# When rider queries, extra keys and LayerNorm rows are transposed in a segment-recurrent attention kernel, and how its instruction pages are counted

## The chip, the cores and the metric

The kernel runs on one core of one Trainium2 chip. The metric is the device time of the whole program in microseconds: a median over several executions. A core has TensorE (matmuls, which write to PSUM), VectorE, ScalarE, GpSimd and SyncE; the last two issue most of the DMA transfers here. Each engine runs its own instruction stream in order, and the streams meet only at semaphores.

## What is computed

The reference is one transformer layer on 2048 tokens of width 640. Its first half is an attention with a recurrent memory: the tokens are cut into 64 segments of 32, each is preceded by 8 memory rows, and the first 8 rows of a segment's attention output are the memory of the next one. So the segments have to be done one after the other. Its second half is a gated feed-forward block.

```python
mem = mem0                                             # 8 rows
for s in range(64):
    h = concatenate([mem, layernorm(x)[32*s : 32*s+32]])   # 40 rows of 640
    q, k, v = h @ Wq, h @ Wk, h @ Wv                   # 32 heads of 128
    p = softmax(mask(q @ k.T / sqrt(128)))
    o = (p @ v) @ Wo
    mem = o[:8]
    outs.append(o[8:])
h = x + concatenate(outs)
out = h + (relu(n @ W_gate) * (n @ W_up)) @ W_down     # n = layernorm(h)
```

## The kernel before

All weights of the attention stay in SBUF. The program is written out in full, segment by segment (the loop at L895), into a list of operations with what each reads and writes. `solve` derives the semaphore waits from that list, and every engine then runs its own operations in the order in which they were added. So the order of the source is the order of each engine, and the order of the SyncE queue in particular is the order in which the DMAs were added.

**One step.** The only thing that depends on the step before is the memory: 8 rows. A matmul on 8 rows costs TensorE as much as one on 32, so the other 24 columns of each projection pass carry "riders": LayerNorm rows of tokens that come one to three segments later. Segment s projects memory s and 24 rider tokens. Four steps bring 96 rider tokens but use up 128, and the missing 32 of every 128 are projected as "extra tokens" in the gaps of three of four steps (`extra_units`, L848): their keys when s % 4 is 2, their queries when it is 3, their values when it is 0. "Kind" below is s % 4.

A step runs on TensorE in this order: K projection into banks 0 and 1, Q projection, first part of the V projection, `pick_mem` (L447, takes the memory queries out of the Q tokens), rest of V, `scores` (L560), the extra projection in five parts (`filler`, L966) with the memory's attention between them, `wo_pass` (L636, the output projection, 128 short matmuls at L642, which gives the next memory), then `pv_x` (L670), the attention of the 32 tokens.

**Token buffers and transposes.** A projection comes out with tokens on the partitions, while scores need the head dimension there. So each result is copied out of PSUM into a token buffer (`to_tok`, L427) and transposed by a DMA on the SyncE queue (`dma_t`, L360). There are four buffers of 512 columns: K goes through `tok` 0 and 1 into `KS`, Q through `tok` 2 and 3 into `QS`. ScalarE copies the even buffers and VectorE the odd ones. From `KS` and `QS` the riders' part is copied into the rings `Kr` and `Qr` (`evac_k`, `evac_q`), where they wait for their segment. `KS` itself is read by this step's scores. The extra tokens' keys and queries are copied by ScalarE into `tok` 2 and 3 (`evac`, L864) and transposed into `Kr` or `QS`.

**When the queries' transpose is issued.** `trans_q` (L456) is issued early, right after the Q copies, in steps of kinds 2 and 3. In kinds 0 and 1 (`qlate`, L938) it is issued after the step's output projection and the first copy of the new memory (L1000), and its copy into `Qr` follows in the next step (`late_k`).

**LayerNorm rows.** Rows of x are loaded into `xt`, scaled by VectorE (`row_scale`, L985), and transposed into `at` (L1005), from where GpSimd copies them into the passes' operand buffers (`ln1_back`). This happens in kind 2, and in kind 0 after steps 31, 35, 39 and 43 for rows of the second half of the layer (`e2b`). `at` also holds, earlier in kinds 1 and 2, the sum of an extra output projection on its way to memory.

**Instruction pages.** TensorE's instructions are fetched in pages of 256 (`PE_LINE`). A matmul is two instructions (weight load and multiply) or, where it keeps its weights, one. `align` (L136) walks through TensorE's operations, keeps the count `at`, and turns some kept weights back into loads (`spare`), so that a page boundary falls a set number of instructions (`MARKS`) after the start of each step's output projection. Waits count too: an instruction can carry one wait, and the others go into separate instructions of up to two waits each. `align` counts one for every wait after the first.

Of the kernel before, what the change touches and what calls it, by code (L numbers as in the profile page):

```python
# [41 lines left out]
class _Graph:  # L42
# [93 lines left out]
    def align(self, first, line):  # L136

        at, spare = first, []  # L140
        for op in self.ops:
            if op.eng != "pe":
                continue
            if op.mark is not None:
                p = (-(at + op.mark)) % line
                room = sum(o.spare[1] for o in spare)
                if p <= room:
                    at += p
                    for o in reversed(spare):
                        o.spare[0] = min(p, o.spare[1])  # L150
                        p -= o.spare[0]
                spare = []
            c = _Count()
            op.fn(c)
            at += c.n + max(0, len(op.waits) - 1)
            if op.spare is not None:
                spare.append(op)

# [48 lines left out]
def build_kernel(nc, A_x, A_mem0, A_Wq, A_Wk, A_Wv, A_Wo, A_seg_len, B_W_gate, B_W_up, B_W_down, out):  # L207
# [15 lines left out]
    VW = 130  # L223
    RING = 96
    PE_FIRST, PE_LINE = 64, 256
    MARKS = (150, 98, 114, 130)

    x_ap, out_ap, mem0_ap = A_x[0], out[0], A_mem0[0]
    h_d = nc.dram_tensor("h_d", [TB, D], BF16)
# [74 lines left out]
    BQ = (0, 1)  # L304
# [55 lines left out]
    def dma_t(dst, src, r, w):  # L360
        add("sp", lambda e: e.dma_start_transpose(dst, src), r=r, w=w, dma=True)
# [65 lines left out]
    def to_tok(b, t, eng):  # L427
        copy_op(eng, tok[t][:, :], bank(b), [B(b)], [("tok", t)])
# [419 lines left out]
    def extra_units(s):  # L848

        b, r = (s - 2) // 4, (s - 2) % 4
        t0 = 64 + 128 * b + 96
        if b < 0 or r == 3 or t0 >= S:
            return None, None, None
        a, ks = act_e[b % 2], [("acte", b % 2)]
        q = seg_slot(t0 // SEG)
        j = (1, 0, 2)[r]

        def part(n):
            project(a, ks, j, (0, 1), BQ, PARTS[n], j // 2)

        def evac():  # L864
            for i, e in enumerate(("act", "act")):
                if j == 2:
                    to_v(BQ[i], Vr[q], i, ("Vr", q), e)
                else:
                    to_tok(BQ[i], 2 + i, e)
            if j == 1:  # L870
                dma_t(Kr[q][:].rearrange("p h t -> p (h t)").rearrange("p (k r) -> p k r", r=128), tokp[1][:, :],
                      [("tok", 2), ("tok", 3)], [("Kr", q)])

        def fin():
            trans_q()
            late_q.append(lambda: evac_q(QS, ("QS",), t0, 32, 0, "act"))
        return part, evac, (fin if j == 0 else None)
# [17 lines left out]
    for s in range(NSEG):  # L895
        last = s == NSEG - 1
        q = seg_slot(s)
        nb = s // 4 + 1
        ln = 64 + 128 * nb < S

        e2 = EARLY.index(s // 4 * 4 + 3) if s // 4 * 4 + 3 in EARLY else None
        e2b = EARLY.index(s - 1) if s - 1 in EARLY else None
        def loads(s=s, e2=e2, e2b=e2b, nb=nb, ln=ln):
            if s % 4 == 3 and e2 is not None:
                dma(xt[:, :], x_ap[128 * e2:128 * e2 + 128, :], r=[("KS",)], w=[("xt",)])
                load_attn(at, e2, [], ("at",))
            if s % 4 == 0 and ln and e2b is None:
                ln1_load(nb, xt, ("xt",))
            if s % 4 == 1 and s - 2 in EARLY:
                e = EARLY.index(s - 2)  # L910
                dma(xn2_d[e], at[:, :], r=[("at",)], w=[("xn2_d", e)])
                if ln:
                    ln1_load(nb, xt, ("xt",))
        if s == 0:
            loads()
        if s > 0:
            a, ks, kn = pass_act(s)
            t0, nr = rider_tokens(s)
            project(a, ks, 1, (0, 1), BQ, (0, 1), spare=16)
            ks = ks + kn  # L920
            project(a, ks, 1, (0, 1), BQ, (2, 3, 4), spare=24)
            to_tok(BQ[0], 0, "act")
            to_tok(BQ[1], 1, "dve")
            if last:
                break
            dma_t(KS[:].rearrange("p h t -> p (h t)").rearrange("p (k r) -> p k r", r=128), tokp[0][:, :],
                  [("tok", 0), ("tok", 1)], [("KS",)])
            trans_ox()
            for f in late:
                f()  # L930
            late = []
            project(a, ks, 0, (0, 1), (P0, P1), spare=40)
            to_tok(P0, 2, "act")
            to_tok(P1, 3, "dve")
            for f in late_k + late_q:
                f()
            late_k, late_q = [], []
            qlate = nr and s % 4 < 2  # L938
            if nr and not qlate and s < NSEG - 2:
                trans_q()  # L940
            loads()
            project(a, ks, 2, (0, 1), (P2, P3), (0, 1), spare=16)
            if s == NSEG - 2:
                trans8(tok[2], ("tok", 2), tok[3], ("tok", 3), T0)
                copy_op("dve", Qr[:, :, q, 0:M], slots(T0, 0, M), [B(T0)], [("Qm", q)])
                evac_q(slots(T0, 0, SEG), B(T0), t0, nr, M, "act")
            else:
                pick_mem(T0)
                copy_op("dve", Qr[:, :, q, 0:M], bank(T0)[:, 0:256].rearrange("p (h t) -> p h t", t=M), [B(T0)], [("Qm", q)])
            if nr:  # L950
                evac_k(KS, ("KS",), t0, nr, M, "dve")
            project(a, ks, 2, (0, 1), (P2, P3), (2, 3, 4), spare=24)
            to_v(P3, Vp, 1, ("Vp", 3), "dve")
            to_v(P2, Vp, 0, ("Vp", 0), "act", 0, 2)
            scores(s)
            exp_mem()
            to_v(P2, Vp, 0, ("Vp", 1), "act", 2, 4)
            exp_x()
            if nr:
                v_riders(t0, nr)  # L960
                if s < NSEG - 2 and not qlate:
                    evac_q(QS, ("QS",), t0, nr, M, "act")
        units, evac, nfin = extra_units(s)
        woe = s % 4 == 1 and s >= 5

        def filler(n):  # L966
            if units:
                units(n)
            if woe:
                woe_pass(BQ[0], WPARTS[n])  # L970
        filler(0)
        filler(1)
        pv_mem(s)
        if s % 4 == 1 and s >= 5:
            copy_op("dve", oTn[:, :, :], oT[:, :, 0:M], [("oT", "m"), ("oT", "n")], [("oTn",)])
        elif s > 0:
            copy_oTe(s - 1)
        norm_om()
        filler(2)
        filler(3)  # L980
        trans_om(128 if s % 4 < 2 else 32)
        mask_x()
        n = n_rows(nb) if s % 4 == 2 and ln else 128 if e2b is not None else 0
        if n:
            row_scale(xt, ("xt",), n, xt, ("xt",))  # L985
        filler(4)
        if evac:
            evac()
        if woe:
            copy_op("dve", oTe[:, :, 0:M], oTn[:, :, :], [("oTn",)], [("oTe", 0)])  # L990
            woe_sum(BQ[0])
            late.append(lambda b=s // 4 - 1: woe_store(b, [("KS",)]))
        wo_pass(T1, MARKS[s % 4] if s > 0 else None)
        if s == NSEG - 2:
            load_gate_up([("oTe", (s - 1) % 4), ("go", T1, 0)])
        to_act(s + 1, B(T1), bank(T1)[:, 0:160])
        if s >= 1:
            wo_rows(T1, wtok[s % 2], ("wtok", s % 2), "act")
            store_attn(wtok[s % 2], ("wtok", s % 2), s - 1)
            if qlate and s < NSEG - 2:  # L1000
                trans_q([("act", (s + 1) // 4 % 2, (s + 1) % 4, "m")])
                late_k.append(lambda t0=t0, nr=nr: evac_q(QS, ("QS",), t0, nr, M, "act"))
        pv_x(s, P0)
        if n:
            dma_t(chunks_of(at[:, :])[:, :, 0:n], xt[0:n, :], [("xt",)], [("at",)])  # L1005
            if s % 4 == 2:
                late.append(lambda nb=nb: ln1_back(nb, chunks_of(at[:, :]), [("at",)], "pool"))
        if nfin:
            nfin()
        norm_x(P0)  # L1010
        if s % 4 == 1 and ln:
            late.append(lambda nb=nb: row_stats(xt, ("xt",), n_rows(nb)))
        if s % 4 == 3 and e2 is not None:
            def f(e2=e2):
                add_attn(xt[:, :], xt, at, [("xt",), ("at",)], [("xt",)])
                dma(h_d[128 * e2:128 * e2 + 128, :], xt[:, :], r=[("xt",)], w=[("h_d", e2)])
                row_moments(xt, ("xt",), 128)
            late.append(f)
            late_q.append(lambda: row_rstd(128))
# [204 lines left out]
```

The softmax here doesn't subtract the row's maximum and nothing guards it: scores larger than these inputs give would overflow.

## Time and profile before

The three timed executions took 1107.77, 1101.67 and 1106.10 us; the median is 1106.1. The profiled execution's span is 1105.2 us, at a mean granted clock of 0.992.

| part of the page | what it says |
|---|---|
| largest TensorE groups | projections L420 and L398, 401.1 and 361.8 us; output projection L642, 156.5 us in 8064 matmuls of 234 ns |
| SyncE's transposes | QS 76, KS 62, oT 62, at 19, Kr 15, xn2T 12 |
| DMA queues | SyncE's own queue 265,776 packets, 41.6% of the 16 engines' span; GpSimd's queue 19,312 packets, 9.5% |
| GpSimd's transfers | Vr<-Vp 376, attn_d<-wtok 62, attn_d<-at 32 |
| chain that ended last | projections 24% and 24%, output projection 13%, FFN gate and up 11%; KS<-tok 2% |

In the lines of groups, the count after x is the number of instructions, then comes the time in which at least one of them ran, then the mean length of one in ns. A transpose is shown on SPq, SyncE's queue, with the time that its issue took; when its data has landed is told separately. "Idle before <- X" is the time that an engine stood still before an instruction and what seems to have ended it; "issue" means that the profile shows nothing that it waited for. Several groups of matmuls run side by side on 32 columns each, so the length of one matmul is not the distance between two.

### The profile page before, as it was taken

Reading aid. Unit: us, or ns where it says so; the run is one execution under the profiler, and the core shown is the slowest. Engines: PE = TensorE matmul, PEld = TensorE weight load, DVE = VectorE, ACT = ScalarE, POOL = GpSimd, SP = SyncE. Lnnn points to the kernel's source line nnn. Section 1 sums busy time; section 2 is a strip of 40 time slices with the busy share of each in tenths; the row PEclk is TensorE's granted clock in tenths of the full one; section 3 lists DMA queues with packets and bytes.
Section 4 is the critical chain, followed back from the end, with each engine's and each line's share of the span. In section 5 each row is a group of like instructions: output and inputs, shape, how many; then the busy total and the mean of one; then the engine's idle time right before and its main releaser. Section 6 shows DMA issues by size and latency. Waiting matters only on the chain.

```text
span 1105.2 us, 55764 instructions
## 1 busy us (share of the span) xinstructions
PE 1054.6 (95%) x27862; PEld 505.9 (46%) x23270; DVE 608.0 (55%) x1673; ACT 362.9 (33%) x792; POOL 290.8 (26%) x585
## 2 busy tenths in 40 slices
PE   4689999999999999999999999999999989999998
PEld 3344444454544444444454444444444455444443
DVE  3245656565656565666666666555656553563422
ACT  1214343333333333333333333333333332131220
POOL 1023333332323232323232324242324152000000
PEclk9989999999999999999999999999999999999999
DMA  9936464545465546567566666464555557222100
GB/s 362 388 92 111 87 104 89 104 91 102 89 100 93 100 89 105 95 107 114 109 111 113 105 117 107 96 99 84 94 108 95 79 148 249 43 78 78 25 18 25
DMA packets 285739, 121.61 MB, mean 110 GB/s; under 512 B 261376, under 2 KB 275156, under 8 KB 285504
## 3 DMA queue, kind: packets, MB, share of 16 engines
q1 hardware_dynamic: 265776, 93.92, 41.6%
q0 software_dynamic: 19312, 23.86, 9.5%
q8 instruction: 201, 3.29, 1.2%
q14 instruction: 34, 0.28, 0.1%
q10 hardware_dynamic: 416, 0.26, 0.1%
HBM read 36.79 MB, written 7.19 MB: 40 GB/s over the span
## 4 chain that ended last, share of the span: by engine, by line
PE 90%; DMA 5%; SPq 3%; issue 1%; DVE 1%; ACT 0%; DVEq 0%
PE ps L420 24%; PE ps L398 24%; PE ps L642 13%; PE ps L1036 11%; PE ps L680 3%; PE ps L656 3%; PE ps L570 3%; PE ps L1068 3%; SPq L358 3%; DMA Wo<-in_A_Wo_dram 3%; PE ps L607 2%; DMA KS<-tok 2%; PE ps L451 2%; PE ps L622 1%; PE ps L1091 1%
## 5 line engine op out<-in xcount | busy, mean ns | idle before, releaser
L420 PE MATMUL ps<-W,act_r 128*32 128x512 bf16 x4261 | 401.1, 387 | 6.6 <-DMA W<-in_A_Wv_dram 2.7
L398 PE MATMUL ps<-W,act_r 128*32 128x512 bf16 x3619 | 361.8, 379 | 1.5 <-issue 1.5
L358 POOL DMA_DIRECT2D Vr<-Vp x376 | 187.2, 505 | 353.3 <-ACT Px L589 288.4
L420 PEld LDWEIGHTS ps<-W,act_r 128*32 128x32 bf16 x4261 | 120.6, 98 | 263.6 <-issue 173.2
L462 ACT ACTIVATE tok<-ps 128x512 bf16<-128x512 f32 x192 | 110.9, 594 | 231.6 <-PE ps L398 205.3
L642 PE MATMUL ps<-Wo,oT 128*32 128x160 bf16 x8064 | 156.5, 234 | 11.2 <-DMA Wo<-in_A_Wo_dram 6.3
L464 DVE CAST tok<-ps 128x512 bf16<-128x512 f32 x131 | 90.6, 691 | 129.7 <-PE ps L398 111.0
L642 PEld LDWEIGHTS ps<-Wo,oT 128*32 128x32 bf16 x8064 | 142.7, 97 | 32.1 <-DVE oT L464 16.9
L420 PE MATMUL ps<-W,act_e 128*32 128x512 bf16 x900 | 90.0, 381 | 2.6 <-issue 2.6
L398 PE MATMUL ps<-W,act_e 128*32 128x512 bf16 x900 | 89.4, 379 | 0.0
L553 DVE STREAM_TRANSPOSE TBf<-ps 128x64 f32<-128x64 f32 (+1 forms) x128 | 33.6, 263 | 94.6 <-PE ps L642 94.6
L695 DVE TENSOR_TENSOR ox<-ps,rx 128x512 bf16<-128x512 f32 x128 | 82.5, 686 | 2.2
L358 POOL DMA_DIRECT2D attn_d<-wtok x62 | 46.3, 748 | 133.0 <-ACT wtok L462 133.0
L462 ACT ACTIVATE Qr<-QS 128x512 bf16<-128x512 bf16 (+3 forms) x107 | 69.7, 680 | 33.1 <-DMA QS<-tok 32.8
L462 ACT ACTIVATE Vp<-ps 128x256 bf16<-128x256 f32 (+1 forms) x126 | 48.5, 385 | 81.4 <-PE ps L398 78.9
L1036 PE MATMUL ps<-xn2T,Wg 128*128 128x512 bf16 x260 | 64.6, 380 | 0.0
L1036 PE MATMUL ps<-xn2T,Wu 128*128 128x512 bf16 x260 | 64.6, 379 | 0.0
L1051 DVE TENSOR_TENSOR hT<-g,ps 128x512 bf16<-128x512 bf16 (+1 forms) x56 | 38.5, 688 | 47.2 <-PE ps L1036 43.4
L1049 ACT ACTIVATE g<-ps 128x512 bf16<-128x512 f32 (+1 forms) x56 | 32.4, 592 | 91.6 <-PE ps L1036 91.6
L398 PE MATMUL ps<-Wd,hT 128*128 128x320 bf16 x224 | 61.0, 300 | 0.0
L1068 PE MATMUL ps<-Wd,hT 128*128 128x320 bf16 x224 | 61.0, 300 | 0.0
L464 DVE CAST Vp<-ps 128x512 bf16<-128x512 f32 x64 | 44.2, 691 | 27.8 <-PE ps L398 21.2
(117 smaller groups left out, 1147.5 us busy)
## 6 DMA issues: line engine op xcount, KB each, us to landing
Vr<-Vp POOLq DMA_DIRECT2D x124, 48.8 KB, 1.9
W<-in_A_Wk_dram SPq DMA_DIRECT2D x2, 2560.0 KB, 13.2
W<-in_A_Wq_dram SPq DMA_DIRECT2D x2, 2560.0 KB, 29.0
W<-in_A_Wv_dram SPq DMA_DIRECT2D x2, 2560.0 KB, 27.9
Wo<-in_A_Wo_dram SPq DMA_DIRECT2D x2, 2560.0 KB, 28.5
xt<-in_A_x_dram SPq DMA_DIRECT2D x30, 160.0 KB, 2.5
Vr<-Vp POOLq DMA_DIRECT2D x128, 32.5 KB, 2.5
at<-attn_d SPq DMA_DIRECT2D x16, 160.0 KB, 3.7
```

Source lines behind the costliest of these rows:

```text
L358: add(eng, lambda e: e.dma_start(dst, src), r=r, w=w, dma=True)
L398: return pe.add_instruction(mybir.InstMatmult(name=nc.get_next_instruction_name(), engine=mybir.EngineType.PE, ins=[pe.lower_ap(rhs), pe.l ...
L420: ins = pe.matmul(*a, start=(c == 0), stop=(c == DC - 1), skip_group_check=True)
L462: add("act", lambda a: a.activation(dst, src, ACTF.Copy), r=r, w=w)
L464: add("dve", lambda v: v.tensor_copy(dst, src), r=r, w=w)
L553: add("dve", lambda v, lo=lo, hi=hi: v.transpose(TBf[:, lo:hi, :].rearrange("p c t -> p (c t)"), src[:, 32 * lo:32 * hi]), r=[wkey], w=[(" ...
L570: i = pe.matmul(bank((P0, P1)[g % 2])[p:p + (M if a else 32), 40 * k:40 * k + 40], lh, Qr[:, h, q, :], start=True, stop=True, skip_group_c ...
L642: i = pe.matmul(bank(bk)[32 * gg:32 * gg + 32, 0:160], src[:, hb, :], w[:, gg], start=(hb == ORDER[0]), stop=(hb == ORDER[31]), skip_group ...
L695: add("dve", lambda v, kh=kh: v.tensor_tensor(ox[:, :, kh, :], src[:, :, kh, 0:128], ap(rx, kh, [[2, 4], [0, 128]]), ALU.mult), r=[B(b0 + ...
L1036: ins = pe.matmul(bank(bk), w[:, c, lo:lo + 128], xn2T[par][:, :, c, :], start=(c == 0), stop=(c == DC - 1))
L1051: add("dve", lambda v: v.tensor_tensor(hT[par][lo:128, j, :], g1[gi][lo:128, :], bank(bu)[lo:128, :], ALU.mult), r=[B(bu), ("g1", gi)], w= ...
L1068: i = pe.matmul(*a, start=(j == 0), stop=(j == FC - 1), skip_group_check=True)
```

## The change

There are four parts.

1. In steps of kind 2 too the rider queries' transpose is issued late, after the output projection. Until it has read them, `tok` 2 and 3 have to keep the step's queries.
2. Since `tok` 2 and 3 are then taken, the extra keys (kind 2) are copied into `tok` 0 and 1, K's buffers, and transposed from there. The extra queries (kind 3) keep 2 and 3.
3. The transpose of the LayerNorm rows is added right behind their scaling, ahead of the extra tokens' and the queries' transposes. In kind 2 SyncE's order changes from KS, oT, QS, Kr, at to KS, oT, at, Kr, QS.
4. `align` counts half as many instructions as an operation has waits, rounded down, and the four marks are set 10 higher. This changes which matmuls load their weights again and takes nine weight loads away from the start of the program.

The purpose is to take the queries' transpose out of the middle of kind 2, to have the rows out of the way of the next step's keys, and to hold the page boundary at one place in every output projection.

```diff
-            at += c.n + max(0, len(op.waits) - 1)
+            at += c.n + len(op.waits) // 2
...
-    MARKS = (150, 98, 114, 130)
+    MARKS = (160, 108, 124, 140)
...
                 if j == 2:
                     to_v(BQ[i], Vr[q], i, ("Vr", q), e)
                 else:
-                    to_tok(BQ[i], 2 + i, e)
+                    to_tok(BQ[i], 2 * (1 - j) + i, e)
             if j == 1:
-                dma_t(Kr[q][:].rearrange("p h t -> p (h t)").rearrange("p (k r) -> p k r", r=128), tokp[1][:, :],
-                      [("tok", 2), ("tok", 3)], [("Kr", q)])
+                dma_t(Kr[q][:].rearrange("p h t -> p (h t)").rearrange("p (k r) -> p k r", r=128), tokp[0][:, :],
+                      [("tok", 0), ("tok", 1)], [("Kr", q)])
...
-            qlate = nr and s % 4 < 2
+            qlate = nr and s % 4 < 3
...
         if n:
             row_scale(xt, ("xt",), n, xt, ("xt",))
+            dma_t(chunks_of(at[:, :])[:, :, 0:n], xt[0:n, :], [("xt",)], [("at",)])
...
         if n:
-            dma_t(chunks_of(at[:, :])[:, :, 0:n], xt[0:n, :], [("xt",)], [("at",)])
             if s % 4 == 2:
```

## The prediction

> **What bounds the kernel now.** I began with the page: busy times, then the chain that ended last.
>
> ```profile
> PE 1054.6 (95%) x27862; PEld 505.9 (46%) x23270; DVE 608.0 (55%) x1673; ACT 362.9 (33%) x792; POOL 290.8 (26%) x585
> ...
> q8 instruction: 201, 3.29, 1.2%
> ...
> PE 90%; DMA 5%; SPq 3%; issue 1%; DVE 1%; ACT 0%; DVEq 0%
> ```
>
> TensorE sets the end. The change removes no matmul, so it can only win or lose idle time of TensorE. Steps 1 to 61 take 829 us together (matmul starts in the timeline), 13.59 each; the fastest of each kind ("kind" is the step's number modulo 4) takes 13.21, 13.29, 13.24 and 13.09 us. With every step at its kind's fastest the sum is 806, so 23 us are there to be won at most. To place them I took the distance between neighbouring matmul starts and compared it with the commonest distance at the same place in steps of the same kind. Two causes remain.
>
> The first is instruction fetch. Queue 8 moves 201 packets of 16 KB, 256 instructions each; TensorE's program has 51,397 instructions, 200.8 such pages. This is its timeline around the end of step 30, whose output projection is L642 (128 matmuls):
>
> ```profile
> 463.28 1.28 PE L642 MATMUL ps<-Wo,oT 128*32 128x160 bf16 x62
> 464.96 1.35 PE L642 MATMUL ps<-Wo,oT 128*32 128x160 bf16 x66 [0.40 <-issue]
> ...
> 468.81 0.39 PE L398 MATMUL ps<-W,act_r 128*32 128x512 bf16 x4
> 470.18 0.40 PE L420 MATMUL ps<-W,act_r 128*32 128x512 bf16 x4 [0.97 <-DVE tok L464]
> ```
>
> Both holes fall where my count of the program puts a page boundary (the "DVE tok" in the second is only the latest event). In the packet records of queue 8 a fetch starts 0.4 to 2.5 us after the boundary before, takes 0.88 to 1.58 us, and where TensorE stalls it resumes 1.2 to 1.7 us after the packet ended. So two boundaries must lie (delay + 1.1 + 1.4) us apart. From scores to output projection they lie 4.0 us apart; the mean delay after the scores is 0.93 us in kind 1, 1.17 in kind 0, 1.44 in kind 3, but 1.55 in kind 2. Stalls in all: output projection 3.6 us in ten kind-2 steps, 1.6 in kind 3, 1.4 in kind 0, 1.1 in kind 1; K projection 3.2 in kind 3, 0.9 in kind 2; scores 3.1 in steps 51 and 59. Sum 14.9.
>
> What delays a fetch is a transpose. SyncE's timeline for the same stretch:
>
> ```profile
> 459.09 1.23 SPq L361 DMA_TRANSPOSE QS<-tok  x1
> 464.63 1.23 SPq L361 DMA_TRANSPOSE Kr<-tok  x1
> 465.97 1.36 SPq L361 DMA_TRANSPOSE at<-xt  x1
> 469.96 1.23 SPq L361 DMA_TRANSPOSE KS<-tok  x1
> ```
>
> A transpose's 1,024 packets run from 1.1 to 2.5 us after its issue. QS occupies the DMA engines at 460.3 to 461.6; the scores' boundary is at 460.33, and its fetch starts at 462.26, when they are free. Kr and at do the same to the boundary at 464.9: fetch at 467.4.
>
> The second cause is the wait of the scores for KS: 0.2 to 0.9 us in steps 33, 37, 41, 45 and 49 (2.8 us), 0.8 us in steps 7, 27 and 43. The chain shows the first:
>
> ```profile
> 497.60 4.57 DMA KS<-tok
> 502.31 0.66 PE ps L570 x63
> ```
>
> In steps 33 to 45 the transpose of at was issued 1.3 us into the step and landed at 6.2 to 6.8, across KS, which landed at 7.2 to 7.6 where the scores want it by 6.8. The page's DMA issues give the landings:
>
> ```profile
> QS<-tok SPq DMA_TRANSPOSE x76, 3.1
> KS<-tok SPq DMA_TRANSPOSE x62, 3.2
> ...
> at<-xt SPq DMA_TRANSPOSE x19, 4.8
> Kr<-tok SPq DMA_TRANSPOSE x15, 5.3
> ```
>
> **What the Trainium skill says.** "Runtime: NRT & Kernel Launch", section "Instruction fetch mechanics": pages of 256 instructions in 16 KiB are fetched by the sequencer's own DMA queue while the page before runs, and the cost is mostly hidden. The page size agrees; "mostly hidden" holds for 144 of the 182 boundaries in these steps, the other 38 cost the 14.9 us. "DMA: Bandwidth & Descriptors", section "Queues, rings and completion order": an engine takes turns between queues packet by packet, and a semaphore's increment lands only after that engine's earlier writes. That agrees: in step 6 a fetch ran 9.32 to 10.80 us into the step, and QS, whose data was through at 9.0, wrote its last 4-byte packet at 11.25 and landed at 11.9.
>
> **The change part by part.**
>
> (a) QS of kind 2 goes behind the output projection. Its packets leave the scores' boundary, so the fetch delay should become that of kinds 0 and 1, about 1.05: need 1.05 + 2.5 = 3.55 against 4.0 apart. Of 3.6 us at the output projection I expect 3.3 to go. ScalarE's two Qr copies (0.63 and 0.40 us at 9.2 to 10.1) move to the next step at about 5.1 to 6.1, between the Q token copy and the Vp copy at 7.1: hidden, as in kinds 0 and 1 today.
>
> (b) Without that stall kind 2's output boundary comes at 11.3 and its fetch at about 12.1, before the first packet of at (issue 11.65 + 1.1 = 12.75; the store out of at that must land first was issued at 7.0 and 7.6 and took 4.2 to 4.6 us across QS, so it may hold at to 11.8). So the kind-3 K stalls should go: 2.7 of 3.2 us. The stalls at the scores of 51 and 59 followed from late K boundaries (fetch 3.8 us later, behind KS, oT and QS); I count half, 1.5.
>
> (c) The row transpose goes first. In steps 32 to 44 it is issued at about 11.6, 3 us sooner, and lands near 16.4, that is 3.1 us into the next step, before KS's packets at 4.2. Of 2.8 us, 2.6 go (49 is another case). In kind 2 it no longer reaches KS of kind 3: 0.8 more.
>
> (d) Kr leaves through tok 0 and 1. This adds a wait: in kind 3 ScalarE's and VectorE's K token copies, today 2.38 us into the step, may not overwrite those buffers before Kr landed. Queued behind them are the Q token copies (4.54), and KS's transpose waits for them, then oT and QS. Kr is issued behind at, at 13.0 (11.65 + 1.36), which is 0.24 us before the next step. Bounds of its landing: 3.1 us as for a lone transpose, 2.9 into the step; 5.3, today's median, 5.1 into it. oT right behind KS lands 0.9 us after it; at, with Vr's writes around it, lands at best near 15.5 like step 3's QS (3.5 to 4.2 after issue); so I take Kr at 16.4, 3.2 into the step. The copies run 0.8 us late, KS lands 0.8 us late at about 7.0, and its slack of 0.5 leaves 0.2 to 0.3 us of wait. Fifteen times 0.2: 3 us. At the upper bound it is 2.7 late, 2.2 us each, 33 us.
>
> (e) QS is then third in the queue: issue at 14.3, 1.0 into the step, landing 4.1 to 5.1; the Q token copies want it by 4.54. Up to 0.6 us, but the same time as (d), since the later wait absorbs the earlier.
>
> (f) Count and marks. The old rule counted one wait instruction too many for each operation with three waits, so the boundary crept through the output projection (kind 0: from the 145th instruction to the 173rd; kind 1: 98 to 126). By my count of the new program it stays at 154, 105, 118 and 130, about the middle of the old paths. The stalls do not follow the place: kind 1 has them at 104 and 108 and none at 96 to 102 or 110 to 126. I cost it at nothing, with plus or minus 1 us. Nine fewer weight loads at the start lie in the wait for weights.
>
> Sum: -3.3 - 2.7 - 1.5 - 2.6 - 0.8 + 3 = -7.9 us, 1098.
>
> **The rivals.** *The new wait takes all back* (Kr at 3.7 into the step, QS landing at 5.3 because a fetch cuts into it): 15 times 0.7 to 0.8 us, 11 us, 1106. For it speak at's 4.8 and the fetch that would start 3 us into kind 3, inside QS's packets. *Slower:* Kr lands as late as today; 15 times 2.2 less 10.9 is +22 us, 1128; halfway, 15 times 1.5 less 10.9, is +12 us, 1118. For it speaks the measured 5.3; against it that the three Kr issued alone (13.7 to 13.9 us into steps 6, 26, 54) landed in 3.0 to 3.1 us, and that the 5.3 came with a fetch that the transposes had held back. *Everything fits:* no new wait, all fetch stalls of kinds 2 and 3 gone: -10.9 - 1.5 - 0.9, 1093.
>
> **How the numbers follow.** Likeliest 1098 with 0.40, everything fits 0.18, taken back 0.24, slower 0.18. The before runs spread from 1101.7 to 1107.8, which blurs each case by 3 us. Below 1100.6 counts as faster: 0.57; within 0.5% 0.26; slower 0.17. The range runs from the best case less the blur, 1089, to short of the halfway case, 1116.
>
> **What would show it.** Right: no hole in L642 of kind 2; KS landing by 6.4 in steps 33 to 45; at issued before Kr; Kr landing 3 to 3.5 us after its issue; token copies of kind 3 at about 3.2. Wrong: ScalarE's and VectorE's token copies waiting for Kr for over 1.5 us in kind 3, or L451 waiting for them after QS, fifteen times, with steps of 14 us or more.

## The result, and the profile after

The changed kernel takes 1144.4 us (median of 4 runs, 1142.0 to 1147.1) against 1104.5 us for the kernel before (4 runs, 1101.7 to 1107.8). The ratio is 1.036, with a 95% interval of 1.032 to 1.041. The prediction was 1098 us with a range to 1116: it was wrong in direction and by 46 us. (A ratio here and below leaves disturbed runs out, so it can differ a little from the quotient of two medians.)

The page of the changed kernel, with the lines that answer to those of before: busy times, the instruction queue, and the chain that ended last by engine and by line.

```profile
PE 1057.4 (93%) x27862; PEld 510.3 (45%) x23292; DVE 607.8 (53%) x1673; ACT 360.7 (32%) x792; POOL 290.4 (25%) x585
...
q8 instruction: 201, 3.29, 1.2%
...
PE 79%; DMA 14%; SPq 3%; DVE 3%; issue 1%; ACT 0%; DVEq 0%
PE ps L420 20%; PE ps L398 19%; PE ps L642 13%; PE ps L1036 10%; DMA Kr<-tok 5%; DMA KS<-tok 4%; PE ps L656 3%; DMA QS<-tok 3%; PE ps L570 3%; PE ps L1068 3%; SPq L358 3%; DMA Wo<-in_A_Wo_dram 2%; PE ps L680 2%; PE ps L607 2%; PE ps L451 1%
```

TensorE does the same 27,862 matmuls and is busy for 3 us more; the span grew by 35 us. So TensorE stands still for longer, and the chain says for what: transfers have gone from 5% of it to 14%, with Kr, which was not among them, at their head.

Added up by kind from the matmul starts, steps 1 to 61 took 829.0 us before and 865.7 after:

| | kind 0 | kind 1 | kind 2 | kind 3 |
|---|---|---|---|---|
| before | 200.0 | 217.9 | 204.6 | 206.5 |
| after | 200.6 | 218.9 | 199.7 | 246.5 |

Kind 2, where the change was made, gained 4.9 us. Kind 3, the step behind it, lost 40.0 us, on average 2.7 us in each of its fifteen steps. Both can be seen in one place. This is TensorE's timeline from the output projection of step 30 (kind 2) into step 31 (start, length, instruction, and the idle time before it):

```profile
483.51 2.40 PE L642 MATMUL ps<-Wo,oT 128*32 128x160 bf16 x128
...
491.45 0.39 PE L398 MATMUL ps<-W,act_r 128*32 128x512 bf16 x4
494.54 0.37 PE L451 MATMUL ps<-ident,tok 128*128 128x32 bf16 x8 [2.71 <-DVE tok L464]
```

The hole in the middle of L642, which the prediction showed for the same step before, is gone: 128 matmuls in one piece. Instead there is a hole of 2.71 us ahead of L451, which needs the Q tokens. SyncE's timeline of the same stretch has the three transposes that the change put there:

```profile
484.90 2.44 SPq L361 DMA_TRANSPOSE at<-xt  x1
487.39 1.32 SPq L361 DMA_TRANSPOSE Kr<-tok  x1
488.75 1.77 SPq L361 DMA_TRANSPOSE QS<-tok  x1
493.77 1.23 SPq L361 DMA_TRANSPOSE KS<-tok  x1
```

And the chain of waits through that hole, in order of time (start, length, what):

```profile
487.39 5.57 DMA Kr<-tok
...
493.05 0.69 DVE tok L464
...
493.77 3.13 DMA KS<-tok
...
497.04 0.72 PE ps L570 x42
```

Kr is issued 0.9 us into step 31 (which begins at 486.47) and lands 5.57 us later; only then can the K tokens be copied, the Q tokens behind them, and KS be issued. KS is issued 7.3 us into the step, where the kernel before issues it at 3.1. Over the whole kernel, the waits and the landings say the same (waiting engine and line, what it waited for: us in total, times, longest; then transposes with their median us from issue to landing):

```profile
ACT tok L462 <- DMA Kr<-tok: 80.5, 15, 6.2
DVE tok L464 <- DMA Kr<-tok: 61.1, 15, 4.9
```

```profile
KS<-tok SPq DMA_TRANSPOSE x62, 3.2
at<-xt SPq DMA_TRANSPOSE x19, 4.3
Kr<-tok SPq DMA_TRANSPOSE x15, 5.6
```

Fifteen waits for Kr, one in each step of kind 3. In the kernel before, Kr took 5.3 us too, but nobody waited for it. (A view's landing times leave out a few transposes whose semaphore records are incomplete; figures below that name all fifteen steps include them.)

### The profile page after: what moved, and what is told of

Its sections match the earlier page's. It is cut to its first block, busy times and chain, and to the rows that moved or that the text cites. A ratio compares the mean times of both kernels' runs of the same rounds, so it can differ in the third digit from the quotient of the medians.

```text
span 1140.4 us, 55786 instructions
## 1 busy us (share of the span) xinstructions
PE 1057.4 (93%) x27862; PEld 510.3 (45%) x23292; DVE 607.8 (53%) x1673; ACT 360.7 (32%) x792; POOL 290.4 (25%) x585
## 4 chain that ended last, share of the span: by engine, by line
PE 79%; DMA 14%; SPq 3%; DVE 3%; issue 1%; ACT 0%; DVEq 0%
PE ps L420 20%; PE ps L398 19%; PE ps L642 13%; PE ps L1036 10%; DMA Kr<-tok 5%; DMA KS<-tok 4%; PE ps L656 3%; DMA QS<-tok 3%; PE ps L570 3%; PE ps L1068 3%; SPq L358 3%; DMA Wo<-in_A_Wo_dram 2%; PE ps L680 2%; PE ps L607 2%; PE ps L451 1%; PE ps L622 1%
## 5 line engine op out<-in xcount | busy, mean ns | idle before, releaser
L420 PEld LDWEIGHTS ps<-W,act_r 128*32 128x32 bf16 x4292 | 122.9, 97 | 258.7 <-issue 164.1
L642 PE MATMUL ps<-Wo,oT 128*32 128x160 bf16 x8064 | 159.6, 237 | 9.9 <-DMA Wo<-in_A_Wo_dram 7.2
L642 PEld LDWEIGHTS ps<-Wo,oT 128*32 128x32 bf16 x8064 | 145.9, 98 | 30.5 <-DVE oT L464 16.2
```

Of the source, the lines that this page charges most:

```text
L420: ins = pe.matmul(*a, start=(c == 0), stop=(c == DC - 1), skip_group_check=True)
L642: i = pe.matmul(bank(bk)[32 * gg:32 * gg + 32, 0:160], src[:, hb, :], w[:, gg], start=(hb == ORDER[0]), stop=(hb == ORDER[31]), skip_group ...
```

## The experiments

Two theories were on the table after this profile. W: the wait for Kr's buffer is all. C: the three transposes in a row crowd the DMA engines, and QS and KS would be late anyway. When both had lost some of their ground, C was split: C1 (the rider values' writes slow the transposes), T (it is the third transpose), F (an instruction fetch that meets a transpose's packets holds up the whole transpose), and G (anything at this seam is slow, wherever the fetch is).

All runs in one table: the median time, the ratio to runs of the kernel before taken beside it (medians 1104.4 to 1105.3) with its interval, and the sums of steps 1 to 61 by kind in the profiled run. The profiled run is one of those timed and can lie away from their median: 1112.7 for e3, 1121.9 for n3.

| run | us | ratio | kind 0 | kind 1 | kind 2 | kind 3 |
|---|---|---|---|---|---|---|
| after | 1144.4 | 1.036 (1.032 to 1.041) | 200.6 | 218.9 | 199.7 | 246.5 |
| e1 own buffer | 1139.5 | 1.031 (1.027 to 1.035) | 199.7 | 219.2 | 199.5 | 244.9 |
| e2 rows last | 1128.4 | 1.020 (1.015 to 1.025) | 199.4 | 220.1 | 199.9 | 233.2 |
| e3 rows first alone | 1122.4 | 1.012 (1.006 to 1.019) | 199.6 | 218.8 | 203.7 | 213.3 |
| e4 count and marks alone | 1101.9 | 0.997 (0.995 to 0.999) | 199.8 | 219.9 | 205.4 | 204.7 |
| e5 own buffer, rows last | 1117.4 | 1.011 (1.008 to 1.015) | 199.4 | 216.9 | 200.8 | 222.9 |
| e6 no rider values | 1151.5 | 1.042 (1.038 to 1.046) | 198.6 | 222.8 | 201.5 | 252.9 |
| e7 rows not transposed | 1127.5 | 1.020 (1.016 to 1.024) | 199.7 | 223.3 | 201.1 | 230.4 |
| e8 fetch 48 later | 1170.3 | 1.062 (1.052 to 1.071) | 208.5 | 228.1 | 200.0 | 252.5 |
| e9 e1, fetch 48 later | 1160.1 | 1.052 (1.045 to 1.060) | 214.0 | 229.9 | 201.2 | 239.6 |
| e10 e5, Kr held back | 1125.3 | 1.017 (1.011 to 1.024) | 199.6 | 217.9 | 201.1 | 234.8 |
| n1 queries mid-step | 1146.5 | 1.040 (1.035 to 1.045) | 199.0 | 218.7 | 235.7 | 214.9 |
| n2 rows first in kind 0 | 1106.5 | 1.001 (0.999 to 1.004) | 200.3 | 225.1 | 203.7 | 204.5 |
| n3 e4, fetch 32 later | 1129.0 | 1.025 (1.016 to 1.033) | 207.0 | 226.1 | 202.2 | 207.4 |
| n4 readers moved | 1123.1 | 1.015 (1.011 to 1.020) | 204.1 | 219.6 | 200.9 | 224.5 |
| n5 n4, Kr held back | 1118.1 | 1.012 (1.007 to 1.018) | 203.6 | 217.2 | 200.9 | 217.9 |

**A buffer of its own for the extra keys (e1).** The extra keys go through `tokx`, so that the K token copies have nothing to wait for. `oTn` lies in the same bytes, since the two are never alive together.

```diff
+    tokx = ar.alloc("tokx", [128, 1024], BF16)
...
+                elif j == 1:
+                    copy_op(e, tokx[:, 512 * i:512 * i + 512], bank(BQ[i]), [B(BQ[i])], [("tokx", i)])
...
-                dma_t(Kr[q][:]..., tokp[0][:, :], [("tok", 0), ("tok", 1)], [("Kr", q)])
+                dma_t(Kr[q][:]..., tokx[:, :], [("tokx", 0), ("tokx", 1)], [("Kr", q)])
```

> The changed kernel with one difference: the extra keys leave through a buffer of their own, so no token copy waits for Kr any more (the small tile oTn, used one step earlier, shares that buffer). Theory W (the loss is the token copies' wait for Kr): kind-3 steps come back from 16.4 us to about 13.4 us, 15 times 3 us, and the gains of kinds 1 and 2 stay: 1094 to 1100 us, faster than before. Rival C (three transposes and the riders' writes crowd the DMA engines, so KS and QS land late whoever waits): kind-3 steps stay above 15 us, 1125 us or more.

It came out at 1139.5, so W fell. The wait has only changed its name; these are the waits of this run:

```profile
ACT tok L463 <- DMA QS<-tok: 68.8, 18, 5.1
DVE tok L465 <- DMA QS<-tok: 67.0, 18, 5.0
```

Now the Q token copies wait for QS, which is behind Kr in the queue and lands 6.7 us into kind 3 (median), where they are due at 4.54.

**Which part costs what (e2, e3, e4).** e2 puts the rows' transpose back behind Kr and QS; e3 is the kernel before with the rows first and nothing else; e4 is the kernel before with the exact count and the new marks.

```diff
# e2, on the changed kernel; e3 is the reverse, on the kernel before
-            dma_t(chunks_of(at[:, :])[:, :, 0:n], xt[0:n, :], [("xt",)], [("at",)])
         filler(4)
...
         if n:
+            dma_t(chunks_of(at[:, :])[:, :, 0:n], xt[0:n, :], [("xt",)], [("at",)])
# e4, on the kernel before
-            at += c.n + max(0, len(op.waits) - 1)
+            at += c.n + len(op.waits) // 2
-    MARKS = (150, 98, 114, 130)
+    MARKS = (160, 108, 124, 140)
```

> The changed kernel with the LayerNorm rows' transpose back at its old place, behind Kr and QS. If the rows in front make Kr late (issue 1.7 to 2.3 us later and a slow landing), Kr is issued at 11.6 us again, lands 3.5 to 5.3 us later, 1.9 to 3.7 us into kind 3, and its steps take 13.4 to 14.3 us: 1100 to 1112 us. If the rows are not the cause (Kr is late because QS follows it and the buffer is K's), nothing much changes: 1130 to 1145 us.

> The kernel before with the rows' transpose first and nothing else: QS of kind 2 stays early, Kr stays in tok 2 and 3. If the rows in front make Kr late by themselves, Kr is issued near 0.5 us into kind 3 and lands at 4 to 6 us; the Q token copies want tok 2 and 3 at 4.5 us, so up to 1.5 us of wait in 15 steps: 1105 to 1125 us. If Kr is late only together with the late QS, it lands by 4.5 us and the gain in kind 1 (2.6 us) shows: 1099 to 1103 us.

> The kernel before with the exact count and the marks 10 higher, nothing else. Theory: the place of the page boundary doesn't matter within these bounds, 1102 to 1107 us like before. Rival: the boundary's place sets the fetch stalls; then the ratio differs from 1 by over 0.5 per cent.

e2 fell between its two branches, e3 into the first of its own, e4 at the edge of the first. Counting up from the kernel before: count and marks take 3 us off (0.3%); rows first, alone, costs 14 us (1.2%) and gives nothing in kind 1, for which it was meant; rows first on top of the late queries costs 16 us (1144.4 less 1128.4). In e3 the Q token copies wait for Kr, whose source is their buffer in that kernel (25.8 and 26.5 us in nine steps), because Kr, now behind the rows, lands 5.3 us into kind 3 (median) instead of 3.5.

**Late queries without the other two (e5).** e1 and e2 together: a buffer of its own and the rows last.

> The changed kernel with a buffer of its own for the extra keys and with the rows' transpose back behind Kr and QS: of the four edits only the late QS and the exact count are left. The first four runs felled W in its pure form (own buffer alone: 1139.5). What is open now is which transposes crowd. L, the late QS is enough: with Kr, QS and at one behind the other the Q token copies of kind 3, due at 4.54 us, wait for a QS that lands at 6 to 7 us (as in the run with rows last), KS is issued at 5 us and lands at 7.5 to 8: some 1.2 us in each of fifteen steps, 1115 to 1125. S, it takes the pair (rows first makes Kr late, or QS late, and the shared buffer turns Kr's lateness into a wait): with each taken away nothing waits beyond 0.5 us in kind 3, and kind 2's output stalls stay away: 1097 to 1102.

1117.4: L, the late QS is enough (with the buffer of its own, which was not tried without it). Against e4 it wins 4.6 us in kind 2 and loses 18.2 in kind 3. QS lands 6.0 us into kind 3. The shared buffer costs 11 us on top of this (e2 less e5), the rows first 16 more.

**Is it the rider values' writes, or the third transpose (e6, e7)?** e6 is the changed kernel without GpSimd's writes of rider values in kind 2 from step 8 on, so the rider rows of Vr keep old values. In e7 VectorE copies the rows of kind 2 untransposed from step 6 on, so LayerNorm's rows are wrong and SyncE has two transposes instead of three.

```diff
# e6
-                v_riders(t0, nr)
+                if s % 4 != 2 or s < 8:
+                    v_riders(t0, nr)
# e7
+            if s % 4 != 2 or s < 6:
                 dma_t(chunks_of(at[:, :])[:, :, 0:n], xt[0:n, :], [("xt",)], [("at",)])
+            else:
+                copy_op("dve", at[0:n, :], xt[0:n, :], [("xt",)], [("at",)])
```

> The changed kernel without the writes of the rider tokens' values into Vr in kind 2 from step 8 on (those rows of Vr keep old values). C1, these small writes on the DMA queues slow the transposes of at, Kr and QS: without them each lands 3.1 to 3.3 us after its issue, Kr at 3.5 us into kind 3, and the time falls to about 1105. F, it is the instruction fetch that meets the burst of packets (in the packet records one engine's 16 KB page freezes the whole transpose): landings stay at 5 to 6.6 us and the time at 1135 to 1145.

> The changed kernel in which the rows of kind 2 from step 6 on are copied untransposed by VectorE instead of transposed (so that LayerNorm gets wrong rows); the transpose at<-xt of kind 2 is gone from the DMA queue. T, it is the third transpose in a row that makes the crowd, since it delays Kr's issue by its own issue and pushes its packets onto the next fetch: Kr is issued at about 11.6 us of kind 2, lands by 15.5 (2.3 us into kind 3), QS lands by 4.5: 1098 to 1106. F, the fetch behind the output projection's boundary meets whatever burst is there: Kr lands 5 us or more after its issue, the K token copies wait for it till 3.5 us or later: 1112 to 1130.

Without the writes the transposes of the rows are quicker and Kr is not; the landings of e6:

```profile
at<-xt SPq DMA_TRANSPOSE x19, 3.4
Kr<-tok SPq DMA_TRANSPOSE x15, 5.8
```

So C1 fell as what makes Kr late, though for the rows the writes count for 0.9 us. At 1151.5 e6 is slower than either branch said; why it is slower than the changed kernel is not shown. T fell too: in e7 Kr is first in the queue, issued at 11.9, and still lands 5.5 us later (median), 3.9 us into kind 3. The time is 1127.5, so the third transpose costs 17 us, but Kr is late without it. What was left is F or G.

**Moving the fetch (e8, e9, n3).** Other marks shift every page boundary of TensorE's program by the same number of instructions; nothing else changes but 48 or 32 weight loads at the start. e8 shifts the changed kernel by 48, e9 shifts e1 by 48, n3 shifts e4 by 32.

```diff
# e8, e9
-    MARKS = (160, 108, 124, 140)
+    MARKS = (-48, -100, -84, -68)
# n3
-    MARKS = (160, 108, 124, 140)
+    MARKS = (-64, -116, -100, -84)
```

> The changed kernel with all page boundaries of TensorE's program 48 instructions later (other marks, so 48 weight loads fewer at the start; nothing else). In kind 2 the boundary in the output projection moves from 11.28 to 11.73 us, the next one from 1.31 to 3.47 us into kind 3. F, a fetch that meets a transpose's burst is what makes Kr late: the fetch behind 3.47 (from 16.7 us of kind 2 on) can no longer meet the packets of Kr (13.9 to 15.2) and of QS (15.4 to 16.7), so Kr lands 2.5 to 3.5 us into kind 3 instead of 5.6, its K token copies run at 3 to 3.6, kind 3 takes 14 to 14.8 instead of 16.4 and the time falls to 1110 to 1125 (some of it lost again where boundaries are now 3.3 us apart). G, the transposes slow each other and the stores, wherever the fetch is: Kr lands at 5 to 6.5 as before and the time stays at 1138 to 1150.

> The same shift of 48 instructions on the changed kernel with a buffer of its own for the extra keys (1139.5 without the shift; there QS, landing at 5 to 7 us, held the Q token copies). F: QS's packets (15.4 to 16.7 us) are free of the fetch too, QS lands at 4 to 5 us into kind 3, the token copies wait for nothing over 0.5 us: 1098 to 1112. G: QS as late as before, 1133 to 1145.

> The kernel before with the exact count and all boundaries 32 instructions later than the change's marks put them (kind 2: scores 7.41 and output 11.59 instead of 7.28 and 11.28, 4.2 us apart instead of 4.0; kind 3: K projection at 3.03, scores 7.85, output 11.53). If the distance between two boundaries sets the stalls: fewer at kind 2's output, as many at kind 0's and 1's (3.5 and 3.4 us apart instead of 4.2 and 3.7): 1097 to 1103. If the fetches then meet KS's and QS's bursts in kind 3 (KS 4.2 to 5.5): 1104 to 1112.

All three came out slower than either branch said. Two things happened. First, the fetch did not go where I had put it: in step 14 of e8 the output projection's fetch starts only at 13.41 us, when most of the rows' packets are through, runs to 14.59 and so meets Kr's, which begin at 14.02. Kr took 5.3 us (median), little less than before. Second, the boundaries now lie badly for everything else: the holes of over 0.1 us at page boundaries in steps 2 to 61 add up to about 28 us in e8 and 49 us in e9, where the changed kernel has 10 by the same count, most of those in kinds 0 and 1 ahead of the memory's attention (`pv_mem`, L607) and in the output projection. In n3 they are 27 us, against 16 in e4. So the times decide nothing about F, but they show by themselves that a shift by 32 instructions costs this kernel 2.7% (n3 against e4).

The landings of QS in e9 do speak for F, within one kernel. In eight of its fifteen steps no fetch ran between the issue of QS and its landing, and it landed 3.3 to 3.7 us after its issue. In the other seven a fetch started 1.7 to 2.3 us after the issue, and it took 4.8 to 5.2 us.

**The same transpose, issued later (e10).** This decided against G. In e5 the extra keys' transpose is issued at about 11.6 us of kind 2, just before the output projection's fetch (which starts at 11.8 to 12.9 and ends at 13.0 to 13.9). e10 holds it until the output projection has ended.

```diff
-                dma_t(Kr[q][:]..., tokx[:, :], [("tokx", 0), ("tokx", 1)], [("Kr", q)])
...
+        def kr():
+            dma_t(Kr[q][:]..., tokx[:, :], [("tokx", 0), ("tokx", 1), ("go", T1, 1)], [("Kr", q)])
...
         wo_pass(T1, MARKS[s % 4] if s > 0 else None)
...
+        if krf:
+            krf()
```

> The run with own buffer and rows last (1117.4), in which the extra keys' transpose also waits for the end of the output projection, so that it is issued at about 13.1 us of kind 2 instead of 11.6. F, the fetch behind the output projection's boundary (12.0 to 13.3 us) is what makes Kr late: Kr lands 3.1 to 3.5 us after its issue, at 16.3 to 16.6, no later than with the earlier issue (16.4 to 17.4). QS then follows at 14.4 and meets the next fetch (from 15.2 us), so the time hardly moves: 1112 to 1122. G, any transpose at the seam of kinds 2 and 3 takes 5 us, whatever the fetch does: Kr lands at 18.2 to 18.6 (5 us into kind 3), QS a little behind, Q token copies later than in e5: 1125 to 1140.

The landings of Kr, first in e5, then in e10 (the view of the tile Kr: us from issue to landing):

```profile
DMA to landing us min/median/max: 5.0/5.3/6.7
```

```profile
DMA to landing us min/median/max: 3.1/3.2/3.7
```

Every one of the fifteen went from 5.0 us or more to 3.7 or less. Issued 1.1 us later, Kr lands *earlier*: at 15.8 to 16.9 us of kind 2 instead of 16.5 to 18.9. Its packets (in step 6 from 13.85 to 15.2) now lie between the end of one fetch (12.9 to 14.0) and the beginning of the next (16.6 and later). F holds for Kr, and G fell. One rival is left: e10 also moves Kr away from GpSimd's rider writes, of which 8 to 15 packets run beside Kr's in e5 and 3 to 7 in e10, so the pair does not say whether the fetch does it alone. n3 says that rider writes are not needed: in nine of its steps Kr is issued after 12.9 us, when no rider write is left. Where the next fetch started 3.48 us or more after the issue (four steps), Kr took 3.1 to 3.3 us; where it started 3.15 to 3.38 us after it (five), just before the landing, 5.1 to 5.8.

The time rose all the same, from 1117.4 to 1125.3, out of F's range: QS, behind Kr, is issued at 13.9 to 14.6 and meets that next fetch. In step 6 its packets run from 15.2 beside the store of attn_d; the fetch starts at 16.6, and packets that had taken 0.03 us take up to 1.47; the rest go through from 18.8, and QS lands at 19.5. It lands 6.4 us into kind 3, later than in e5 (6.0), and the Q token copies wait for it there.

**Attempts at a better kernel (n1, n2, n4, n5).** n1 is e4 with the extra keys' own buffer, rows first only in kind 0, and QS of kind 2 issued behind the exp of Px. n2 is e4 with rows first only in kind 0. n4 is e5 in which the main Q tokens of kind 3 go into the extra keys' buffer and the rows of kind 2 are transposed in kind 3 behind KS; n5 is n4 with Kr held back as in e10.

```diff
# n1
+                if qmid and s < NSEG - 2:
+                    trans_q([("Px",)])
# n1, n2
+        if n and e2b is not None:
+            dma_t(chunks_of(at[:, :])[:, :, 0:n], xt[0:n, :], [("xt",)], [("at",)])
# n4, n5
+            tq = TX if s % 4 == 3 and s < NSEG - 2 else TQ
...
+            for f in late_t:
+                f()
```

> A version made from what the runs showed: the kernel before, with the exact count and marks (1101.9 alone), a buffer of its own for the extra keys, the rows' transpose first only in kind 0, and kind 2's QS issued after the exp of Px (about 8.75 us into the step), neither at the scores' boundary nor among Kr and at. If a burst costs only where it meets a fetch: kind 2's output stall goes (-3), KS's wait in kind 1 goes (-2.6), kind 3 stays as before: 1095 to 1099. If every rearrangement of QS only moves the collision: QS at 8.75 holds up the fetch behind the scores' boundary or lands across Vr's writes, stalls of 0.3 us or more at kind 2's output or context projection: 1102 to 1110.

> The kernel before with the exact count and marks (1101.9 alone) and the rows' transpose first only in kind 0 (steps 32 to 44), where it crossed KS of the next step. If that crossing is all: 2 us less, 1098 to 1101. If the rows then meet another fetch or hold QS of kind 1 (QS behind at, as in steps 33 and 41 of the changed kernel): 1101 to 1105.

> Own buffer, late QS in kind 2, and nothing in kind 3 that overwrites what Kr or QS still read: the main Q tokens of kind 3 go into the extra keys' buffer (free once Kr has landed, at 3.5 to 5 us), and the rows' transpose of kind 2 is issued in kind 3 right behind KS. If the token copies' waits and the queue in front of KS are all that took kind 2's gain back: kind 3 near 13.6 us, kind 2 as in the changed kernel (13.2): 1095 to 1100. If the rows behind KS hold oT or QS, or the Qr copies wait for a QS at 6 to 7 us: scores of kind 3 at 7.5 to 8, 1103 to 1112.

> n4 with Kr held until the output projection's end as in e10. F: Kr lands at 16.4, QS behind it; the Q tokens of kind 3 find their buffer free at 3.2 us: as n4 or 1 to 3 us better, 1093 to 1099. G: Kr lands at 5 us into kind 3, the Q copies due at 4.54 wait 0.5 us fifteen times: 5 to 8 us above n4.

None of the four came out within its ranges. n1 says little about its idea, because the edit made a wait of its own: by naming Px as read, the transpose makes VectorE's mask, which writes Px, wait until QS has landed:

```profile
DVE Px L597 <- DMA QS<-tok: 51.0, 15, 4.2
```

n2: QS of kind 0, now behind the rows, is issued 0.3 to 0.6 us into steps 33, 37, 41 and 45, lands at 5.7 to 6.6, and the scores there begin at 8.2 to 9.4 instead of 6.9 to 7.9; kind 1 loses 5 us against e4. In n4 and n5 no token copy of kind 3 waits any more, but the reader behind them does; of n5:

```profile
ACT Qr L466 <- DMA QS<-tokx: 43.7, 15, 3.5
```

In n5 QS lands at 6.0 to 6.7 and the scores start near 7.3, and in some steps (six of kind 3 in n4, four in n5) oT, put behind the rows, lands at 10.8 us or later, which makes them 15.2 to 17.4 us long. In seven (n4) and six (n5) steps of kind 0 the Q token copies now wait for the extra queries' QS, and kind 0 is 4 us longer than in e4. n5 is 5 us better than n4 by the medians, as F said, though their runs overlap (1115.8 to 1123.8 against 1119.8 to 1127.1), and at 1118.1 it is far from 1093 to 1099.

e4, the exact count and marks alone, is the only version that beats the kernel before: 1101.9 us, ratio 0.997 (0.995 to 0.999).

**How far the fetch explains landings in general.** From the traces of all seventeen kernels I took the transposes of steps 1 to 61 whose forerunners had landed by 1.1 us after their issue, and sorted them by when the nearest fetch ended, counted from the issue (the first row reaches back to 0.2 us before it).

| fetch ended | KS over 4 us | Kr over 4 us |
|---|---|---|
| before 1.0 us | 4 of 356 | 4 of 41 |
| 1.0 to 1.8 us | 7 of 300 | 43 of 45 |
| 1.8 to 4.2 us | 9 of 12 | 64 of 64 |

A fetch that is over before the transpose's packets begin, at 1.1 us, seldom costs anything. One that ends late holds up either transpose. But one that ends at 1.0 to 1.8 us holds up Kr and not KS. What differs there is GpSimd: four or more of its data packets run beside 43 of those 45 Kr, and beside one of the 300 KS. So, as far as these traces tell, an early meeting costs much only with other writes beside it, and e5, where the fetch ends 1.4 to 2.3 us after Kr's issue, is mostly such a case. The rule is not exact: with no fetch ending in these stretches, 2 of 114 KS and all 7 Kr took over 4 us. Why the writes matter no run here shows.

The packets themselves are plainer. Over the same traces 17,707 packets of 256 bytes on SyncE's queue took 0.35 us or more in these steps, where 0.02 is usual. 78% of them end between 0.75 and 1.0 us after the end of a fetch packet. Steps 1 to 61 of the kernel before have 182 boundaries in 829 us, one in 4.6 us, so by chance that stretch would hold some 5%.

## Why the prediction was wrong

The mechanism that decides, token copies of kind 3 waiting for Kr, was named in step (d) and again as the slower rival; its size was wrong, and with it the sign of the sum.

(a) held. I expected 3.3 us less at kind 2's output projection; its ten stalls of 3.6 us became one of 0.05, and kind 2 gained 4.9 us.

(b) cannot be told: the long K stalls of kind 3 and those at the scores of steps 51 and 59 are gone, but TensorE now waits in the same steps for the tokens.

(c) failed. The rows are issued at 11.6 and KS of kind 1 lands by 6.6 in steps 33 to 45 (6.4 was predicted, 7.2 to 7.7 it was before), but I did not ask what stands behind the rows in kind 0: it is QS, which then lands 5.5 us into steps 33 and 41 (scores there at 7.9). Instead of 2.6 us less, kind 1 has 1.0 more, and e3 shows the part alone to cost 14 us (n2, its half in kind 0, 4 us against e4).

(d) is the step that failed. "Kr is issued behind at, at 13.0" was 12.9 to 14.3, median 13.6, because the issue of at took 1.9 us (median, up to 2.44), not 1.36. "So I take Kr at 16.4, 3.2 into the step" was 5.0 to 6.6 in fourteen steps, median 6.0. Where I had written fifteen times 0.2 us, 3 us, kind 3 lost 2.7 us a step, 40 us. Most of the error is the landing time: 5.6 us after the issue where I had put 3.4. My bounds were 3.1 us for a lone transpose and 5.3 as measured before; I took a value near the lower one, and the upper one was exceeded (5.6). Two arguments led there. One was that three Kr issued alone had landed in 3.1 us. They were not alone, since at was issued 1.3 us behind each as it was behind most slow ones; they had been issued at 13.5 to 13.9, when the fetch was over or nearly so, and e10 shows that this is enough to make one quick (in e7 Kr is first in the queue and still takes 5.5). The other was that "the 5.3 came with a fetch that the transposes had held back": I had the right suspect, and then assumed that the change would part the two. It did the opposite: the packets of three transposes in a row run from 12.6 us on, and a second fetch starts among them, at 16.1 to 17.7 us. One step shows what was missing. In step 50 Kr's packets were through at 15.9, before the fetch at 16.1, and it landed 3.3 us after its issue; in the other fourteen it took 5.0 to 6.4.

(e) failed with it: QS landed 6.6 us into kind 3, not at 4.1 to 5.1. "The later wait absorbs the earlier" was right, and it is why e1 gained only 5 us.

(f) was close: nothing, plus or minus 1 us, against 0.3% (0.1 to 0.5%, 1 to 5 us) less in e4.

The slower rival had the right form, Kr "as late as today", and 1128; it fell short by 16 us, mostly because a step of kind 3 lost 2.7 us instead of 2.2 (40 us for 33) and because it set 10.9 us of gains against it, of which 4.9 came.

"DMA: Bandwidth & Descriptors" of the Trainium skill, section "Queues, rings and completion order", which the prediction cited, fits what is seen here in part: if an engine takes turns between queues packet by packet, one turn of the fetch is 16 KB (mostly 0.9 to 1.6 us) while a transpose's own packet is 256 bytes (0.02 us). But that explains the share of one engine. In e5's step 6 the flow of the 256-byte packets falls from 164 in 0.2 us to between 7 and 14 for 0.8 us, so more than one of the 16 engines stands, and the wait outlasts the turn: in e7's step 6, 21 of Kr's packets, started between 13.3 and 13.9 us, end at 14.1 to 14.3, where the fetch packet had ended at 13.36. No run here shows why.

## What to carry to other kernels

When a change makes somebody wait for a transfer that nobody waited for, its landing time as measured in place is the estimate; a shorter time measured elsewhere may be used only when it is known what made it shorter, and the same trace can often tell (here: issued before or after the fetch). Lay every burst of transfers and every fetch on one time axis before moving any of them. A burst that leaves one collision goes into the next gap between fetches: if the gap holds it, issuing later can land earlier, as Kr did in e10; if not, it meets the next fetch, as QS did there.

## What the runs showed of the hardware

A transpose of 1,024 packets of 256 bytes lands 3.1 to 3.7 us after its issue when no fetch runs between its first packet and its landing (Kr in e10, fifteen steps), and 4.8 to 5.2 us when an instruction page, one packet of 16 KB, starts 1.7 to 2.3 us after the issue (QS in e9, seven steps against eight at 3.3 to 3.7). A fetch that ends by 1.8 us after the issue left KS alone (11 of 656 over 4 us) and held up Kr where GpSimd wrote beside it. Packets that are held up end together, most of them 0.75 to 1.0 us after the end of a fetch packet, and the transposes queued behind slip too. The issue of a transpose is not a constant either: SyncE's 1.23 us became up to 2.7 us in e7 and 2.44 us for the at of step 30.

In the kernel before, a matmul on 8 columns of loaded weights took 180 ns in the scores where one on 32 took 188.

The placement of TensorE's page boundaries alone is worth more than the whole change was meant to bring: a shift by 32 instructions, 1101.9 against 1129.0 us (ratios 0.997 and 1.025).
